# Attention, a dense layer and routed experts on one core: key and query steps one turn ahead, a second batch turned by VectorE, subtractions given to GpSimd

## Chip, core and metric

The kernel runs on one core of one Trainium2 chip. The metric is the device time of one execution in microseconds. Three runs of the kernel before gave 915.5, 917.96 and 918.49 us, with a median of 917.96 us.

## What is computed

```python
q, k, v: (4, 12, 448, 64)             # batch, heads, sequence, head_dim, float32
scores = q @ k.T / 8 - log(448)
x = sigmoid(scores) @ v               # -> (1792, 768)
h = x @ w_in                          # (768, 2048), float64 in memory
x2 = maximum(0.01 * h, h) @ w_out     # (2048, 768), float64 in memory
e = argmax(x2 @ w_gate)               # one of 8 experts for each token
y = maximum(x2 @ w1[e], 0) @ w2[e]    # (768, 1024), (1024, 768)
out = softmax(x2 @ w_gate)[e] * sigmoid(x2 @ w_ogate)[e] * y
```

Only the attention inputs, the two dense weights, the gates and the expert weights come from memory. All of the output is float32.

## The kernel before, in words

The 1792 tokens are four batches of 448. A batch goes through attention, the dense layer's first product (M1) and second product (M2), a routing step, and two products with the expert that is the commonest in the batch (M3, M4). A short loop at the end serves the tokens that want another expert.

Precise products are made of three fast ones. A tile is split into a hi part (rounded to the fast format) and a lo part (the rest), and `mm3` (lines 361 to 364) adds hi x hi, hi x lo and lo x hi. So each weight chunk of 128x768 or 128x640 is read (`raw`), copied by ScalarE to `whi`, and subtracted to `wlo`. Keys and queries are split in the same way: `kh`, `kl`, `qh`, `ql`.

Keys and queries must first be turned so that the head dimension lies on the partitions. For batches 0 and 1 TensorE does it (`turn`, line 422: four transposes into the PSUM tile `pst`). For batches 2 and 3 the load already lays out 32x32 blocks, and VectorE transposes these (`steps_T`, line 460: `kt`, `qt`).

Two ways of ordering stand side by side:

- `first_batches` (lines 978 to 1302) orders all work of batches 0 and 1 up to the end of batch 0's M2. It is a list of operations with an engine, a planned length and a due time; `_Plan.order` sorts them, and each engine gets its operations in that order. Here 34 chunks of the dense weights also change from float64 to float32: ScalarE makes `dw` from the loaded half chunk (line 1160), VectorE makes `raw` from it in three steps (lines 1165, 1168, 1171), GpSimd's queue stores the chunk for later batches (line 1181), and the chunk is split (lines 1200 and 1204). At the very start `heat` runs products of no use on TensorE (`hot`, line 1006).
- Later batches run as generators. The attention of batches 2 and 3 (`attention`, line 493) is spread over the products of earlier batches by `Filler`: for each step of the products, the attention may spend `ratio` times as much, and it pays with each of its `yield`s. One turn of it is a pair of heads: the scores of two chunks (`sc`, line 439), the previous pair's values (`pv`, line 452), the scores of the other two chunks; then four steps that turn and split the next pair's keys and queries. Routing (`routing`, line 610) goes forward one `yield` at a step of the products, and two in the last batch.

Each engine works through its queue in order; a wait at its head holds all that stands behind.

Of the kernel before, what the change touches and what calls it, by code (L numbers as in the profile page):

```python
# [9 lines left out]
F32 = mybir.dt.float32  # L10
# [8 lines left out]
P = 128  # L19
TP = 112  # L20
NCH = 4
# [98 lines left out]
def kernel(  # L120
# [13 lines left out]
    nc = tc.nc  # L134
# [132 lines left out]
    class Stream:  # L267
# [52 lines left out]
        def next(self):  # L320
            self.stage(2, self.ni)
            self.ahead()
            self.ni += 1
            return self.got.pop(self.ni - 1)
# [62 lines left out]

    SQ = 32

    def load_nat(nm, b, p):  # L390
        src = {"kn": k, "qn": q, "vn": v}[nm]
        if nm == "vn":
            a = nat_p.tile([TP, 2, NCH * D], F32, tag=nm, name=nm)
            if b >= 2:
                nc.sync.dma_start(a.rearrange("p h (c d) -> p h c d", c=NCH), src[b, 2 * p:2 * p + 2].rearrange("h (c p) d -> p h c d", c=NCH))
            else:
                nc.sync.dma_start(a, src[b, 2 * p:2 * p + 2].rearrange("h (p c) d -> p h (c d)", c=NCH))
        elif b >= 2:

            a = nat_p.tile([P, S // SQ, SQ], F32, tag=nm, name=nm)  # L400
            for j in range(P // SQ):
                i, f = divmod(j * SQ, D)
                nc.sync.dma_start(a[j * SQ:(j + 1) * SQ], src[b, 2 * p + i, :, f:f + SQ].rearrange("(n t) d -> t n d", t=SQ))
        else:
            a = nat_p.tile([TP, NCH, 2, D], F32, tag=nm, name=nm)
            for i in range(2):

                how = "(p c) d -> p c d" if nm == "kn" else "(c p) d -> p c d"
                nc.sync.dma_start(a[:, :, i, :], src[b, 2 * p + i].rearrange(how, c=NCH))
        nat[nm, b, p] = a  # L410

    def load_qk(b, p):
# [80 lines left out]
    def attention(b):  # L493


        st = {"at": {}}
        for _ in steps_T(b, 0, st):
            yield 0.4
        ahead_(load_qk, b, 2)
        prev = None  # L500
        for p in range(NP):
            nxt = {"at": {}}
            prep = steps_T(b, p + 1, nxt) if p + 1 < NP else iter(())
            room = None if p % 2 else rows_p.tile([TP, 2, 2, S], F32, tag="rows", name="ats")
            step_S(st, FRONT, room)
            if prev is not None:
                step_V(b, *prev, FRONT + BACK)
            step_S(st, BACK)
            for _ in range(4):
                yield C_E / 2  # L510
                next(prep, None)
            if p + 1 < NP:
                for _ in prep:
                    pass
                ahead_(load_qk, b, p + 3)
            prev = (p, st)
            st = nxt
        step_V(b, *prev, FRONT + BACK)
        yield C_V * 2
# [90 lines left out]
    def routing(b):  # L610
# [31 lines left out]
        yield  # L642
        rows_turn(b, xf[1], 1)
        xf[3] = rows_add(b, 3)
        yield
        yield
        yield
        cp = ps_t.tile([P, NCH, E], F32, tag="t", name="cp")
        nc.tensor.matmul(cp.rearrange("p c e -> p (c e)"), ones[:TP], eq.rearrange("p c e -> p (c e)"), start=True, stop=True)
        cnt = sm("cnt", [P, E])  # L650
# [327 lines left out]
    def first_batches():  # L978
# [4 lines left out]
        V = nc.vector  # L983
        L_QK, L_V, L_W64, L_W, LD_LAT = 1.3, 0.95, 1.55, 1.45, 2.0
        T_A, T_S2, T_V2, T_M = 0.4, 1.4, 1.8, 0.6
        A0 = 8.0
        HEAT = 24
        DEC = (40.0, 5.0)
        A_T = NP * 2 * (T_A + T_S2 + T_V2)
        D0 = A0 + A_T  # L990
# [15 lines left out]
            nc.tensor.matmul(hot.t[:, :P], ident, ident, start=True, stop=True)  # L1006

        for i in range(HEAT):
            pl.add(PE, 0.21, heat, uses=() if i == 0 else (hot,), new=() if i else (hot,), due=1e6)


        nats = {}

        def load(nm, b, p):
            s = pl.slot(nm, 2)
            nats[nm, b, p] = (s, pl.add(DMA, L_V if nm == "vn" else L_QK, lambda: load_nat(nm, b, p), new=(s,), lat=LD_LAT))

        def part(back):
            pv, vs, vop, b, p, at, sg, cs = back
# [17 lines left out]
        def attention_ops(b, t0, step):  # L1037
            for p in range(NP):
                for nm in ("kn", "qn", "vn"):
                    load(nm, b, p)  # L1040
            xs = pl.slot(f"x{b % 2}", 1)
            lows = low_of[b] = []
            behind = None
            for p in range(NP):
                def due(c):
                    return t0 + (p * NCH + c) * step


                stk, ready = {}, []
                for nm in "kq":  # L1050
                    ns, nop = nats[nm + "n", b, p]
                    ring = ("m", 2) if b == 0 and nm == "k" else ("t", 1)
                    ts = pl.slot("ps_" + ring[0], ring[1])
                    h, l = stk[nm] = [pl.slot(nm + x, 2) for x in "hl"]

                    def turn_(nm=nm, ts=ts, ring=ring, b=b, p=p):
                        ts.t = turn(nat.pop((nm + "n", b, p)), {"m": ps_m, "t": ps_t}[ring[0]], ring[0])

                    def thi(nm=nm, ts=ts, h=h):
                        h.t = stk_tile(nm + "h")  # L1060
                        nc.scalar.copy(h.t, ts.t)

                    def tlo(nm=nm, ts=ts, h=h, l=l):
                        l.t = stk_tile(nm + "l")
                        V.tensor_sub(l.t, ts.t, h.t.bitcast(F32))

                    o = pl.add(PE, T_A, turn_, deps=(nop,), uses=(ns,), new=(ts,))
                    o = pl.add(ACT, 0.5, thi, deps=(o,), uses=(ts,), new=(h,))
                    ready += [o, pl.add(DVE, 0.54, tlo, deps=(o,), uses=(ts, h), new=(l,))]
                four = (*stk["k"], *stk["q"])  # L1070
                pv = pl.slot("ps_v", 1)
                vs, vop = nats["vn", b, p]
                at, sg = {}, {}
                for cs in (FRONT, BACK):
                    sc = [pl.slot("ps_s", 2) for _ in cs]
                    new = list(sc)
                    deps, uses = list(ready), list(four)
                    back = behind
                    if cs == BACK:
                        new.append(pv)  # L1080
                        back = (pv, vs, vop, b, p, at, sg, FRONT)
                    if back:
                        deps += [back[2], *(back[6][c] for c in back[7])]
                        uses += [back[1], *(back[5][c] for c in back[7])]
                        if cs == FRONT:
                            uses.append(back[0])

                    def both(cs=cs, sc=sc, four=four, back=back):
                        for s_, t in zip(sc, scores(*(x.t for x in four), cs)):
                            s_.t = t  # L1090
                        if back:
                            part(back)

                    o = pl.add(PE, T_S2 + (T_V2 if back else 0.0), both, deps=deps, uses=uses, new=new, due=due(cs[1]))
                    if back:
                        last = o
                        if cs == FRONT:
                            finish(b, p - 1, back[0], last, xs, lows, due(0))
                    for c, s_ in zip(cs, sc):
                        at[c] = pl.slot("at", 4)  # L1100

                        def sig(s_=s_, a=at[c]):
                            a.t = squash(s_.t)

                        sg[c] = pl.add(ACT, 0.9, sig, deps=(o,), uses=(s_,), new=(at[c],))
                behind = (pv, vs, vop, b, p, at, sg, BACK)

            o = pl.add(PE, T_V2, lambda: part(behind), deps=(behind[2], *(behind[6][c] for c in BACK)),
                       uses=(behind[0], behind[1], *(behind[5][c] for c in BACK)), due=due(NCH) + 2.0)
            finish(b, NP - 1, behind[0], o, xs, lows, due(NCH) + 2.0)  # L1110
            return xs
# [80 lines left out]
        def chunk(j):  # L1192
            kk, n, _ = ws.src[j]
            got = fresh(j)
            hs, ls = his[j], los[j] = pl.slot("hi", 3), pl.slot("lo", 3)
            rs = raws[j]

            def hi():
                hs.t = whi_p.tile([P, kk, n], F32R, tag="hi", name="whi")
                nc.scalar.copy(hs.t, rs.v)  # L1200

            def lo():
                ls.t = wlo_p.tile([P, kk, n], F32R, tag="lo", name="wlo")
                V.tensor_sub(ls.t, rs.v, hs.t.bitcast(F32))  # L1204

            o = pl.add(ACT, 0.73, hi, deps=got, uses=(rs,), new=(hs,))
            return pl.add(DVE, 0.87, lo, deps=(o,), uses=(rs, hs), new=(ls,))


        nm = 0  # L1210
# [90 lines left out]
            ws.got[jj] = (his[jj].t, los[jj].t) if jj < stage[1] else raws[jj].v  # L1301
        gT[0] = None

    A_PE = NP * 2 * C_E + C_V + 1.6
    pace = [1]

    def tick(c):
# [40 lines left out]
    with tc.manual_schedule():  # L1348
        for b in range(0, B, 2):
            for i in range(2):  # L1350
                add_dense(b + i == 0)
            for i in range(2):
                add_exp(b + i)
        consts()
        first_batches()
        for b in range(0, B, 2):
# [59 lines left out]
```

## Time and profile before

| what | value |
|---|---|
| median of three runs | 917.96 us |
| the profiled execution's own time | 917.8 us |
| its span, first to last instruction | 916.2 us |
| TensorE busy | 889.9 us, 97% |
| VectorE busy | 506.1 us, 55% |
| ScalarE busy | 423.2 us, 46% |
| GpSimd busy | 59.4 us, 6% |
| granted TensorE clock, mean | 0.996 |

The span is 1.6 us shorter than the profiled execution's time. Busy time counts a matmul until its modelled end, and matmuls overlap in the pipeline; where one starts can be read from the start column. The list of waits shows for each engine what it stood idle for.

### The profile page before, as it was taken

How to read it: one execution, taken by the hardware profiler on the slowest of the kernel's cores; microseconds unless marked ns; L12 is line 12 of the kernel's file. 1: busy time of each engine (PE TensorE's matmuls, PEld its weight loads, DVE VectorE, ACT ScalarE, POOL GpSimd, SP SyncE). 2: the span in 40 equal slices, each digit the busy share in tenths (PEclk: the TensorE clock that was granted, in tenths of full speed). 3: DMA queues.
4: the chain of work that ended last, by engine and by line, in shares of the span. 5: the costliest groups of instructions: out<-in, count | busy, mean ns of one | idle time of the engine just before them, and what ended most of it. 6: DMA issues, size and time to landing. Idle time of an engine off the chain costs nothing.

```text
span 916.2 us, 13126 instructions
## 1 busy us (share of the span) xinstructions
PE 889.9 (97%) x4660; PEld 742.4 (81%) x4660; DVE 506.1 (55%) x994; ACT 423.2 (46%) x681; POOL 59.4 (6%) x94
## 2 busy tenths in 40 slices
PE   8799999999999999999999999999999999999996
PEld 6357877887899998787678777777989999889885
DVE  3748999852964327554334555432486432775343
ACT  5767676552444223445453656543345332233331
POOL 2000111100020000200000000000002100121000
PEclk9999999999999999999999999999999999999999
DMA  8984878872664333688346744232356434348433
GB/s 184 310 263 136 262 238 269 257 202 67 125 132 130 111 117 78 110 165 168 78 97 136 185 100 103 89 117 64 104 119 136 132 101 127 69 109 183 121 91 68
DMA packets 264773, 129.41 MB, mean 141 GB/s; under 512 B 172984, under 2 KB 249432, under 8 KB 264704
## 3 DMA queue, kind: packets, MB, share of 16 engines
q1 hardware_dynamic: 259584, 115.53, 51.0%
q0 software_dynamic: 4192, 12.89, 3.9%
q8 instruction: 38, 0.62, 0.3%
q14 instruction: 31, 0.25, 0.1%
q10 hardware_dynamic: 928, 0.11, 0.1%
HBM read 104.77 MB, written 23.77 MB: 140 GB/s over the span
## 4 chain that ended last, share of the span: by engine, by line
PE 75%; issue 8%; DVE 8%; DMA 2%; ACT 2%; SPq 0%; POOL 0%; POOLq 0%; ACTq 0%; DVEq 0%
PE psm L362 21%; PE psm L363 20%; PE psm L364 20%; PE pv L452 7%; PE sc L439 6%; DVE wlo L298 1%; DMA r64big<-in_moe_w_in_dram 1%; DMA r64big<-in_moe_w_out_dram 1%; DMA out_dram<-yt 1%; DVE wlo L1204 1%; DVE x2t L591 1%; DVE raw L1168 1%; PE lgT L561 1%; PE lgT L562 1%; DVE raw L1171 1%
## 5 line engine op out<-in xcount | busy, mean ns | idle before, releaser
L298 DVE TENSOR_TENSOR wlo<-raw,whi 128x768 fp32r<-128x768 f32 (+2 forms) x180 | 152.9, 854 | 84.8 <-ACT whi L290 83.3
L362 PE MATMUL psm<-gh,whi 128*128 128x448 f32 x528 | 193.3, 366 | 0.0
L364 PE MATMUL psm<-gh,wlo 128*128 128x448 f32 x528 | 191.1, 362 | 0.3 <-DVE wlo L298 0.3
L363 PE MATMUL psm<-gl,whi 128*128 128x448 f32 x528 | 191.3, 362 | 0.0
L290 ACT CAST whi<-raw 128x768 fp32r<-128x768 f32 (+2 forms) x180 | 135.6, 753 | 85.5 <-PE psm L363 71.9
L362 PEld LDWEIGHTS psm<-gh,whi 128*128 128x128 f32 x528 | 99.1, 188 | 14.4 <-issue 6.9
L362 PE MATMUL psm<-x0h,whi 128*128 128x448 f32 x288 | 107.1, 372 | 0.7 <-ACT x0h L1028 0.6
L362 PE MATMUL psm<-x1h,whi 128*128 128x448 f32 (+1 forms) x288 | 106.1, 369 | 0.0
L364 PEld LDWEIGHTS psm<-gh,wlo 128*128 128x128 f32 x528 | 98.9, 187 | 8.7 <-DVE wlo L298 1.6
L364 PE MATMUL psm<-x1h,wlo 128*128 128x448 f32 (+1 forms) x288 | 105.2, 365 | 0.0
L363 PE MATMUL psm<-x0l,whi 128*128 128x448 f32 x288 | 104.6, 363 | 0.4 <-DVE x0l L1032 0.4
L363 PE MATMUL psm<-x1l,whi 128*128 128x448 f32 (+1 forms) x288 | 104.8, 364 | 0.0
L364 PE MATMUL psm<-x0h,wlo 128*128 128x448 f32 x288 | 104.3, 362 | 0.0
L363 PEld LDWEIGHTS psm<-gl,whi 128*128 128x128 f32 x528 | 99.1, 188 | 5.6
L446 ACT ACTIVATE at<-sc,nbias 112x896 f32<-112x896 f32 x84 | 80.4, 1010 | 15.9 <-PE sc L439 15.7
L452 PE MATMUL pv<-at,vn 112*64 112x448 f32 x336 | 71.0, 550 | 0.0
L362 PEld LDWEIGHTS psm<-x0h,whi 128*128 128x128 f32 x288 | 54.1, 188 | 11.3 <-issue 4.8
L362 PEld LDWEIGHTS psm<-x1h,whi 128*128 128x128 f32 x288 | 54.1, 188 | 5.5 <-issue 0.6
L364 PEld LDWEIGHTS psm<-x1h,wlo 128*128 128x128 f32 x288 | 54.0, 188 | 4.6
L363 PEld LDWEIGHTS psm<-x1l,whi 128*128 128x128 f32 x288 | 54.0, 187 | 4.5
L363 PEld LDWEIGHTS psm<-x0l,whi 128*128 128x128 f32 x288 | 54.1, 188 | 4.1 <-DVE x0l L1032 0.9
L364 PEld LDWEIGHTS psm<-x0h,wlo 128*128 128x128 f32 x288 | 54.0, 187 | 4.0 <-DVE wlo L298 0.2
(218 smaller groups left out, 1051.4 us busy)
## 6 DMA issues: line engine op xcount, KB each, us to landing
raw<-wscr SPq DMA_DIRECT2D x66, 384.0 KB, 3.6
raw<-in_moe_w_dram SPq DMA_DIRECT2D x32, 384.0 KB, 3.9
raw<-in_moe_w_dram SPq DMA_DIRECT2D x48, 256.0 KB, 3.2
raw<-wscr SPq DMA_DIRECT2D x36, 320.0 KB, 2.9
r64big<-in_moe_w_in_dram SPq DMA_DIRECT2D x25, 384.0 KB, 5.3
wscr<-raw POOLq DMA_DIRECT2D x22, 384.0 KB, 5.4
r64big<-in_moe_w_out_dram SPq DMA_DIRECT2D x20, 384.0 KB, 5.3
vn<-in_v_dram SPq DMA_DIRECT2D x24, 224.0 KB, 3.7
```

What stands on the lines that cost most here:

```text
L290: nc.scalar.copy(hi, self.got[i])
L298: nc.vector.tensor_sub(lo, r, hi.bitcast(F32))
L362: nc.tensor.matmul(ps, wh, xh, start=first, stop=False)
L363: nc.tensor.matmul(ps, wh, xl, start=False, stop=False)
L364: nc.tensor.matmul(ps, wl, xh, start=False, stop=last)
L439: nc.tensor.matmul(t[:, i, :S], kk[own, ks], qq[own], start=(n == 0), stop=(n == 2))
L446: nc.scalar.activation(a, sc[:, :, :S], ACTF.Sigmoid, bias=nbias[:TP], scale=scale)
L452: nc.tensor.matmul(pv[own], vn[:, i, c * D:(c + 1) * D], at[c][:, i], start=(c == 0), stop=(c == NCH - 1))
L561: nc.tensor.matmul(lgT[b], wg_c[:, d], xh[:, d, :S], start=(d == 0), stop=False)
L562: nc.tensor.matmul(lgT[b], wg_c[:, d], xl[:, d, :S], start=False, stop=(d == KD - 1))
L591: nc.vector.transpose(t, xf)
L1168: V.scalar_tensor_tensor(t(), w(), 0x80000000, t(), ALU.bitwise_and, ALU.bitwise_or)
```

## The change

1. `TURNED = 1`: batch 1 too is loaded in 32x32 blocks (four DMAs for a key or query tile in place of two) and turned by VectorE (`swing`), so TensorE has 48 transposes less. The values of batch 1 are loaded in the layout of batches 2 and 3.
2. The lo parts of the dense weights within `first_batches` (34 chunks, and two of batch 1's) are subtracted by GpSimd, in the plan with 1.7 in place of VectorE's 0.87.
3. In `attention` a step of the next pair is made before each `yield` and no longer after it; the first pair's steps take 1.5 each in place of 0.4, with one more `yield` behind. `A_PE`, from which `ratio` follows, rises from 41.8 to 49.5.
4. Routing makes five `yield`s before the count `cp`, in place of three.
5. The first key and query tiles are loaded ahead of the constants, half by SyncE's queue and half by ScalarE's. `HEAT` falls from 24 to 14, `A0` from 8 to 6.

```diff
+    TURNED = 1
-    def load_nat(nm, b, p):
+    def load_nat(nm, b, p, by=(nc.sync, nc.sync)):
...
-            if b >= 2:
+            if b >= TURNED:
...
-                nc.sync.dma_start(a[:, :, i, :], src[b, 2 * p + i].rearrange(how, c=NCH))
+                by[i].dma_start(a[:, :, i, :], src[b, 2 * p + i].rearrange(how, c=NCH))
...
         for _ in steps_T(b, 0, st):
-            yield 0.4
+            yield 1.5
+        yield 1.5
...
             for _ in range(4):
+                next(prep, None)
                 yield C_E / 2
-                next(prep, None)
...
         xf[3] = rows_add(b, 3)
-        yield
-        yield
-        yield
+        for _ in range(5):
+            yield
...
-        A0 = 8.0
-        HEAT = 24
+        A0 = 6.0
+        HEAT = 14
...
-            pl.add(PE, 0.21, heat, uses=() if i == 0 else (hot,), new=() if i else (hot,), due=1e6)
+            pl.add(PE, T_A, heat, uses=() if i == 0 else (hot,), new=() if i else (hot,), due=1e6)
...
+                    def swing(nm=nm, ts=ts, b=b, p=p):
+                        ts.t = turn_p.tile([P, S], F32, tag=nm, name=nm + "t")
+                        V.transpose(ts.t, nat.pop((nm + "n", b, p)).rearrange("p n d -> p (n d)"))
...
-                    o = pl.add(PE, T_A, turn_, deps=(nop,), uses=(ns,), new=(ts,))
+                    o = pl.add(*((DVE, 0.6, swing) if own else (PE, T_A, turn_)), deps=(nop,), uses=(ns,), new=(ts,))
...
-                V.tensor_sub(ls.t, rs.v, hs.t.bitcast(F32))
+                nc.gpsimd.tensor_sub(ls.t, rs.v, hs.t.bitcast(F32))
...
-            return pl.add(DVE, 0.87, lo, deps=(o,), uses=(rs, hs), new=(ls,))
+            return pl.add("POOL", 1.7, lo, deps=(o,), uses=(rs, hs), new=(ls,))
...
-    A_PE = NP * 2 * C_E + C_V + 1.6
+    A_PE = NP * 2 * C_E + 2 * C_V + 7.5
...
+        for nm in ("kn", "qn"):
+            load_nat(nm, 0, 0, (nc.sync, nc.scalar))
         consts()
```

At the start TensorE's order before is 16 `hot`, the transposes of `kn`, 4 `hot`, those of `qn`, 4 `hot`, scores; now the `hot` counts are 7, 1 and 5, and the last one stands behind the first scores.

Three places in the order of instructions follow. First ScalarE in batch 0's attention, from the third pair of sigmoids (`at`, two chunks each) on. Before:

```order
L446 ACTIVATE at<-sc,nbias 112x896 x2
L1200 CAST whi<-raw 128x768
L446 ACTIVATE at<-sc,nbias 112x896 x2
L1061 CAST kh<-pst 128x448
L1061 CAST qh<-pst 128x448
L1160 ACTIVATE dw<-r64big 128x384 x3
L1028 CAST x0h<-pv 128x448
L446 ACTIVATE at<-sc,nbias 112x896 x2
```

The same stretch of ScalarE's queue in the changed kernel:

```order
L448 ACTIVATE at<-sc,nbias 112x896 x2
L1171 ACTIVATE dw<-r64big 128x384 x2
L1211 CAST whi<-raw 128x768
L448 ACTIVATE at<-sc,nbias 112x896 x2
L1068 CAST kh<-pst 128x448
L1068 CAST qh<-pst 128x448
L1171 ACTIVATE dw<-r64big 128x384 x2
L1171 ACTIVATE dw<-r64x 128x384
L1211 CAST whi<-raw 128x768
L1034 CAST x0h<-pv 128x448
L448 ACTIVATE at<-sc,nbias 112x896 x2
```

Two conversions of half chunks have moved in front of the fourth pair of sigmoids, and a `whi` in front of the fifth, behind three conversions as before.

Second GpSimd's queue in the changed kernel, from its first work for the weights on; before, only the stores (`wscr<-raw`) stood here, one after another:

```order
L1215 TENSOR_TENSOR wlo<-raw,whi 128x768 x3
L1192 DMA wscr<-raw 128x768 x8
L1215 TENSOR_TENSOR wlo<-raw,whi 128x768 x3
L1192 DMA wscr<-raw 128x768
L1215 TENSOR_TENSOR wlo<-raw,whi 128x768 x2
L1192 DMA wscr<-raw 128x768
```

The subtractions are now between the stores, the first three ahead of all stores.

Third VectorE in batch 2's attention, at the fourth pair of heads, whose queries' lo part is `ql`; `gl` and `wlo` belong to the expert product that runs beside it. Before:

```order
L460 STREAM_TRANSPOSE qt<-qn 128x448
L855 SCALAR_TENSOR_TENSOR gl<-psm,gh 128x448
L298 TENSOR_TENSOR wlo<-raw,whi 128x768
L463 TENSOR_TENSOR ql<-qt,qh 128x448
L482 TENSOR_TENSOR x0l<-pv,x0h 128x448
```

The same pair in the changed kernel:

```order
L462 STREAM_TRANSPOSE qt<-qn 128x448
L857 SCALAR_TENSOR_TENSOR gl<-psm,gh 128x448
L298 TENSOR_TENSOR wlo<-raw,whi 128x768
L465 TENSOR_TENSOR ql<-qt,qh 128x448
L462 STREAM_TRANSPOSE kt<-kn 128x448
L484 TENSOR_TENSOR x0l<-pv,x0h 128x448
```

On VectorE `ql` stands where it stood, but the next pair's `kt` now comes ahead of `x0l`. What the rows cannot show is that a `yield` now lies between `ql` and the scores that read it, so that TensorE has a piece of the product to do between them.

## Rows read from the trace of the kernel before

**Rows 1.** The page: span, and busy time of each engine.
```profile
span 916.2 us, 13126 instructions
PE 889.9 (97%) x4660; PEld 742.4 (81%) x4660; DVE 506.1 (55%) x994; ACT 423.2 (46%) x681; POOL 59.4 (6%) x94
```

**Rows 2.** Waits of TensorE: what it waited for, us, times, longest.
```profile
PE sc L439 <- ACT at L446: 5.1, 3, 4.0
PE sc L439 <- ACT qh L461: 2.8, 2, 1.5
PE sc L439 <- DVE ql L463: 1.9, 3, 1.5
...
PE cp L649 <- DVE eq L641: 1.4, 1, 1.4
...
PE sc L439 <- ACT ats L446: 1.0, 2, 0.5
PE sc L439 <- ACT qh L1061: 0.8, 1, 0.8
...
PE pst L422 <- DVE kl L1065: 0.4, 1, 0.4
```

**Rows 3.** Windows: length, busy of PE, PEld, DVE, ACT, POOL; clock, DMA share, GB/s.
```profile
20.00:40.00 20.00, 14.07 (x86) 7.40 (x88) 14.25 (x28) 15.43 (x24) 2.18 (x4) 0.91 1.03 299
...
80.00:200.00 120.00, 118.77 (x641) 95.22 (x640) 105.07 (x220) 78.74 (x137) 14.44 (x26) 1.00 0.81 247
200.00:217.00 17.00, 17.00 (x90) 13.07 (x88) 5.52 (x7) 6.48 (x9) 0.00 (x0) 1.00 0.26 83
```

**Rows 4.** Timeline of TensorE, first stretch: start, us, instruction, idle before.
```profile
6.92 0.55 PE L422 MATMUL pst<-ident,kn 112*128 112x112 f32 x4
...
8.21 0.55 PE L422 MATMUL pst<-ident,qn 112*128 112x112 f32 x4
...
9.59 0.46 PE L439 MATMUL sc<-qh,kh 64*112 64x448 f32 x2
...
32.82 0.72 PE L439 MATMUL sc<-qh,kh 64*112 64x448 f32 x2 [4.02 <-ACT at L446]
```

**Rows 5.** The two first loads of `qn`, issued at 2.4 and 3.0 us.
```profile
L409 SPq DMA_DIRECT2D qn<-in_q_dram x2: 490/551/612, 2.4 to 3.0; - x2
...
DMA to landing us min/median/max: 2.9/2.9/3.0
```

**Rows 6.** Timeline of ScalarE before the longest wait of TensorE ends.
```profile
30.89 0.55 ACT L1160 ACTIVATE dw<-r64big 128x384 f32<-128x384 f32 x1 [1.41 <-DVE raw L1168]
...
31.76 1.91 ACT L446 ACTIVATE at<-sc,nbias 112x896 f32<-112x896 f32 x2
```

**Rows 7.** Timeline of TensorE around a group of transposes of batch 1.
```profile
108.52 0.55 PE L422 MATMUL pst<-ident,kn 112*128 112x112 f32 x4
108.84 0.45 PE L362 MATMUL psm<-x0h,whi 128*128 128x448 f32 x1
```

**Rows 8.** Timeline of VectorE ahead of the scores of batch 2's fourth pair.
```profile
434.74 0.95 DVE L298 TENSOR_TENSOR wlo<-raw,whi 128x768 fp32r<-128x768 f32 x1
435.61 0.62 DVE L463 TENSOR_TENSOR ql<-qt,qh 128x448 fp32r<-128x448 f32 x1
```

**Rows 9.** Groups of VectorE, 80 to 200 us: count, busy us, mean ns.
```profile
L1204 DVE TENSOR_TENSOR wlo<-raw,whi 128x768 fp32r<-128x768 f32 (+1 forms) x25 | 22.5, 902 | 3.2 <-ACT whi L1200 2.8
...
L1246 DVE TENSOR_TENSOR g<-t,psm 128x448 f32<-128x448 f32 x14 | 8.6, 615 | 0.2
```

**Rows 10.** Line 460: VectorE's transposes, ns min, median, max.
```profile
L460 DVE STREAM_TRANSPOSE kt<-kn x12: 635/638/639, 377.9 to 604.4; 128x448 f32<-128x448 f32 x12
```

**Rows 11.** Timeline of GpSimd: its longest instruction that is no DMA.
```profile
794.85 0.76 POOL L756 MEMSET xm<- 32x769 f32 x1
```

**Rows 12.** DMA issues: count, KB each, median us to landing.
```profile
kn<-in_k_dram SPq DMA_DIRECT2D x24, 112.0 KB, 4.4
...
kn<-in_k_dram SPq DMA_DIRECT2D x48, 56.0 KB, 3.2
```

More of the change, by code (lines that the diff above doesn't have):

```diff
@@ L397, in load_nat @@
                 nc.sync.dma_start(a, src[b, 2 * p:2 * p + 2].rearrange("h (p c) d -> p h (c d)", c=NCH))
-        elif b >= 2:
+        elif b >= TURNED:
             a = nat_p.tile([P, S // SQ, SQ], F32, tag=nm, name=nm)
@@ L1015, in load @@
             s = pl.slot(nm, 2)
-            nats[nm, b, p] = (s, pl.add(DMA, L_V if nm == "vn" else L_QK, lambda: load_nat(nm, b, p), new=(s,), lat=LD_LAT))
+            if (nm, b, p) in nat:
+                o = pl.add(DMA, L_QK / 2, lambda: None, new=(s,), due=0.0, lat=LD_LAT)
+            else:
+                o = pl.add(DMA, L_V if nm == "vn" else L_QK, lambda: load_nat(nm, b, p), new=(s,), lat=LD_LAT)
+            nats[nm, b, p] = (s, o)
         def part(back):
@@ L1051, in attention_ops @@
                     ns, nop = nats[nm + "n", b, p]
-                    ring = ("m", 2) if b == 0 and nm == "k" else ("t", 1)
-                    ts = pl.slot("ps_" + ring[0], ring[1])
+                    own = b >= TURNED
+                    ring = (nm, 1) if own else ("m", 2) if b == 0 and nm == "k" else ("t", 1)
+                    ts = pl.slot(("turn_" if own else "ps_") + ring[0], ring[1])
                     h, l = stk[nm] = [pl.slot(nm + x, 2) for x in "hl"]
```

## The prediction

> **What bounds the kernel now.** I read the page first. TensorE is busy for 889.9 of 916.2 us [rows 1], so the kernel is bound by TensorE, and only two things can shorten it: less work on TensorE, or fewer of the 26.3 us in which it stands idle. A faster VectorE, ScalarE or GpSimd is worth something only where TensorE waits for it.
>
> So the second view is the list of TensorE's waits [rows 2]. The reader is to see that the waits are few and have names. Scores wait 5.1 us for sigmoids (`at`), 4.0 of them at once. Scores of the later batches wait 2.8 us for `qh` and 1.9 us for `ql`. The count `cp` waits 1.4 us. Batch 1's keys and queries cost 0.8 and 0.4 us of waiting. Another 1.0 us goes to `ats`, the first sigmoids of a batch.
>
> The third view is the table of stretches [rows 3]. From 20 to 40 us TensorE is busy for 14.07 of 20 us, with the DMA engines at a share of 1.03: there the transfers are full and TensorE is not. From 80 to 200 us TensorE is busy for 118.77 of 120 us and VectorE for 105.07: VectorE has little left, but TensorE hardly waits for it. From 200 us on VectorE has 11.5 of 17 us free.
>
> **The change part by part.**
>
> *Transposes.* 12 groups of four leave TensorE. A group that starts at 108.52 us is followed by a product at 108.84 [rows 7], so it costs 0.32 us, and 12 x 0.32 = 3.8 us go. VectorE gets 12 transposes of 0.64 us [rows 10] for them. The two waits that belonged to them, 0.8 for `qh` and 0.4 for `kl` [rows 2], can go too, since no PSUM tile is shared any longer; I take 1.0 of 1.2, with 0 and 1.2 as bounds. The loads for them are smaller and twice as many: 56 KB lands after 3.2 us, 112 KB after 4.4 [rows 12]. SyncE issues some 0.55 us a piece [rows 5], so 24 more issues are 13 us of its queue, spread over 200 us, and the conversions of the dense weights stand behind them. They are loaded two pairs ahead, and that hides them; without this cover, within the stretch of full DMA engines, they would cost up to the difference of 2 x 3.2 and 4.4 us, 2.0 us, once. That is within the bounds of the next part.
>
> *The start.* The last `qn` load is issued at 3.0 us and lands 2.9 us later [rows 5], yet its transposes start at 8.21, behind the useless products, and the scores at 9.59 [rows 4]. With half of the issues on ScalarE's queue the last issue is some 1.1 us earlier, and with 8 useless products ahead in place of 20 the transposes can start at 5.5 to 6. I take 2.4 us for that. Behind it stands the wait of 4.0 us, which ends at 32.82 [rows 4]. Its cause is ScalarE's queue: the sigmoids at 31.76 stand behind a conversion that waited 1.41 us for VectorE [rows 6], and that one behind loads. In the new order three conversions and a `whi` stand before the same sigmoids, and two conversions before the pair ahead of them. So I do not take this wait as removed: loads decide it, they come earlier by what the start gives, and the gain may be 0.6 us beyond that. The granted clock is 0.91 over these 20 us, and the matmul pair at 32.82, after 4.02 us of idleness, takes 0.72 us where 0.46 is usual [rows 4]: that is 1.8 us of clock lost at the lower of the two levels, 1.2 in place of 2.4 GHz. Together I take 3.0 us. The bounds are 0 (loads set the pace and the head start is lost) and 8.2 (2.4, the whole 4.0, and the 1.8).
>
> *Subtractions on GpSimd.* VectorE loses 25 of 0.90 us, 22.5 us, between 80 and 200 us [rows 9]. No row shows GpSimd with two inputs. The lower bound is its memset of 769 columns at 0.76 us [rows 11], which only writes; the upper is three times that, 2.3 us, for two reads and a write in turn. I take 1.5, nearer to the memset doubled. GpSimd is busy for 14.44 of these 120 us [rows 3]; 25 x 1.5 = 37.5 us more leave it half idle, and even 57.5 us fit. As VectorE was not what TensorE waited for, the relief is worth nothing by itself. The chunk is ready 0.6 us later than before; three buffers hide that, and I count it once, where the first product starts: +0.6 us.
>
> By the Trainium skill's "GPSIMD Engine Reference", section 3.1, the same operation takes GpSimd 4497 ns where VectorE takes 2293. An estimate from that ratio is 1.8 us for a subtraction here, and the sum with it would be 0.3 us higher.
>
> *One turn ahead.* Scores of the fourth pair wait for `ql`, which runs at 435.61, directly behind a `wlo` [rows 8], because it was given out just before them. Now a `yield` of 1.6 lies between. At the new ratio, `A_PE` over three products of 8 x 6 steps of 0.57 (82.1) by 1.08, 49.5 / 82.1 x 1.08 = 0.65, it is paid with 1.6 / 0.65 = 2.5 us of products. All five long waits of this kind are at most 1.5 us [rows 2], so the work that hides them is longer. 2.8 + 1.9 = 4.7 us go. The bounds are 3.0 (for the pair above `gl` and `wlo` still come first, and half of it may stay) and 5.5. The 1.0 us for `ats` stays, since it is the first turn's own chain of scores and sigmoids.
>
> *Routing.* Two more `yield`s are one step of the products in the last batch, where two are made at a time: three matmuls, 0.6 us of the 1.4. I take 0.6; bounds 0 and 1.4.
>
> **Sum.** 3.8 + 1.0 + 3.0 + 4.7 + 0.6 - 0.6 = 12.5 us less than the profiled execution's own 917.8 us: 905.3. That execution is 0.2 us from the median of the runs shown, so I predict 905.
>
> **The rivals.**
>
> *VectorE and GpSimd shut each other out.* As a mechanism: while GpSimd subtracts, VectorE cannot do what reads two tiles of SBUF. Without the `wlo`, VectorE has 105.07 - 22.5 = 82.6 us of work between 80 and 200 us, and 8 transposes add 5.1: 87.7. With 25 subtractions of 1.5 us that nothing overlaps it is 125.2 us for a stretch of 120, in which chunks already come just in time. That is 5.2 us back, 910.5; I put it at 911. For it speaks that the stretch is the fullest of the kernel on VectorE; against it, that the gains elsewhere stay and that VectorE has room after 200 us.
>
> The Trainium skill, "SBUF — State Buffer", section "Who interferes with whom", states this as a rule: a VectorE instruction with two SBUF inputs contends with a GpSimd instruction that reads SBUF, and the loser waits for the whole instruction. No row here shows the two together, so it bears on this rival alone, and with its sister page's 1.8 us the rival would be at 917.
>
> *Slower than before.* The same place at the upper price. At 2.3 us the sum is 87.7 + 57.5 = 145.2 us, 25 us more than the stretch; with `g` (8.6 us, one input in PSUM [rows 9]) and the transposes running beside it, 11.5. The middle is 18 us: 905 + 18 = 923. It decides from a shut-out of 1.8 us on, where 25 x 1.8 + 87.7 passes 120 by the 12.5 us of the gains. Against it: 0.76 us for 769 columns.
>
> *The head start is lost.* Loads fill the DMA engines at 20 to 40 us; if they set the pace from the first microsecond on, the start brings nothing and the sum is 908.
>
> *Waits only move.* The change does not do what it says: `ql` still comes last behind `gl` and `wlo`, batch 1's transposes on VectorE come behind decoding and scores wait for them. The 4.7 and 1.0 us stay, the start is lost: 914 to 917, say 916. Against it, the covers worked out above.
>
> **How the numbers follow.** Forecast 0.55 (its own range 899 to 910), lost head start 0.13 (908), shut-out 0.17 (911), slower 0.07 (923), waits only move 0.08 (916). The range 897 to 914 holds the first three but for their ends, 0.80. A difference of 0.3%, 2.8 us, is about what a measurement of this kernel can tell from none; so faster means below 915.2: 0.54 + 0.13 + 0.15 + 0.02 = 0.84. Within 0.3%: 0.08. Slower: 0.08.
>
> **What would show it.** In the changed kernel's trace the scores' waits for `qh` and `ql` are gone from TensorE's list. The first scores start at about 7 us in place of 9.59. Transposes of batch 1 stand on VectorE, and the first product of batch 1 (`x1h`) starts some 7 us earlier than before. TensorE still waits for `at` somewhere before 40 us, for 2 to 4 us. GpSimd's subtractions are spaced by 1.5 us where three follow one another, and VectorE is busy for about 88 us of a stretch of the same work. The prediction is wrong if VectorE's other instructions take visibly longer than before while GpSimd subtracts, if TensorE's list has a new wait for `wlo`, or if the stretch up to 40 us ends as late as before.

## The result and the profile after

The changed kernel takes 929.59 us (median of four runs, 927.87 to 930.52); the kernel before, in the four runs beside it, takes 917.61. The ratio is 1.0132, with a 95% interval of 1.0117 to 1.0146. It is slower by 12 us; 905 us was predicted. The profiled execution took 927.87 us.

The page of the changed kernel, to be held against [rows 1]:

```profile
span 926.3 us, 13072 instructions
PE 888.0 (96%) x4592; PEld 739.5 (80%) x4592; DVE 515.9 (56%) x970; ACT 421.0 (45%) x681; POOL 122.7 (13%) x130
```

TensorE is busy 1.9 us less than before and the span is 10.1 us longer, so the time went into waits. One line of the page deserves a second look: VectorE gave away 36 subtractions and took up 12 transposes, yet it is busy for 515.9 us where it was busy for 506.1.

TensorE's list of waits in the changed kernel (what it waited for, us in total, times, longest):

```profile
PE sc L441 <- ACT at L448: 12.4, 6, 4.7
PE psm L362 <- DVE g L1257: 9.4, 5, 3.9
...
PE cp L651 <- DVE eq L644: 0.8, 1, 0.8
```

Against [rows 2], the waits for `qh` and `ql` of the later batches are gone, as predicted, and the count's wait has shrunk from 1.4 to 0.8. But the wait for sigmoids has grown from 5.1 to 12.4 us, and there is a wait that was not there at all: 9.4 us for `g`, the first product's result behind its leak, which VectorE makes.

More than a third of the sigmoid wait is one place: 4.7 us at 54.85 us. ScalarE's sigmoids there stand directly behind this conversion of a half chunk, which waited for its load:

```profile
53.35 0.54 ACT L1171 ACTIVATE dw<-r64big 128x384 f32<-128x384 f32 x1 [3.79 <-DMA r64big<-in_moe_w_in_dram]
```

The table of stretches of the changed kernel (columns as in [rows 3]):

```profile
20.00:40.00 20.00, 13.88 (x81) 6.68 (x80) 16.98 (x26) 15.34 (x25) 5.99 (x4) 0.91 0.98 254
40.00:60.00 20.00, 13.16 (x68) 6.40 (x65) 12.74 (x28) 9.23 (x16) 3.60 (x7) 0.91 0.91 274
...
120.00:140.00 20.00, 15.33 (x75) 11.62 (x74) 16.72 (x26) 12.34 (x22) 7.60 (x7) 0.92 0.64 195
140.00:160.00 20.00, 20.00 (x100) 15.13 (x100) 16.97 (x32) 12.50 (x23) 8.99 (x8) 0.90 0.72 217
...
80.00:200.00 120.00, 108.76 (x554) 85.44 (x550) 107.33 (x186) 72.57 (x128) 54.27 (x45) 0.97 0.69 209
```

From 80 to 200 us TensorE was busy for 118.77 us and now is for 108.76. VectorE, without its 25 subtractions, is still busy for 107.33, and for fewer instructions (186 in place of 220). The granted clock falls to 0.92 and 0.90 between 120 and 160 us.

Where one of the new waits comes from is seen in the timelines around 135 us. TensorE first:

```profile
134.31 0.36 PE L363 MATMUL psm<-x0l,whi 128*128 128x448 f32 x1
134.51 0.36 PE L364 MATMUL psm<-x0h,wlo 128*128 128x448 f32 x1
138.81 0.74 PE L362 MATMUL psm<-x0h,whi 128*128 128x448 f32 x1 [3.94 <-DVE g L1257]
139.35 0.57 PE L363 MATMUL psm<-x0l,whi 128*128 128x448 f32 x1
139.73 0.57 PE L364 MATMUL psm<-x0h,wlo 128*128 128x448 f32 x1
```

VectorE in the same stretch:

```profile
127.39 3.02 DVE L1264 TENSOR_TENSOR gl<-g,gh 128x448 fp32r<-128x448 f32 x1
...
130.87 0.55 DVE L1176 TENSOR_SCALAR raw<-dw 128x384 uint32<-128x384 uint32 x2
...
135.11 0.60 DVE L1076 STREAM_TRANSPOSE qt<-qn 128x448 f32<-128x448 f32 x1
135.64 2.12 DVE L1176 TENSOR_SCALAR raw<-dw 128x384 uint32<-128x384 uint32 x2
137.68 0.55 DVE L1179 SCALAR_TENSOR_TENSOR raw<-dw,raw 128x384 uint32<-128x384 uint32 x1
138.15 0.61 DVE L1257 TENSOR_TENSOR g<-t,psm 128x448 f32<-128x448 f32 x1
```

And GpSimd:

```profile
135.78 1.83 POOL L1215 TENSOR_TENSOR wlo<-raw,whi 128x768 fp32r<-128x768 f32 x1 [0.85 <-ACT whi L1211]
```

VectorE works without a gap from 127.39 us on, so `g` is late only because of what stands ahead of it. The two shifts at 135.64 take 2.12 us; the pair at 130.87, with no subtraction beside it, takes 0.55. They end at 137.76, 0.15 us behind GpSimd's subtraction, which began at 135.78. TensorE then stands for 3.94 us and comes back with matmuls that start 0.38 us apart, where 0.20 was usual. From 137.0 to 143.8 us the granted clock is 0.50: the lower of the two levels, after idleness, as in [rows 4].

### The profile page after: what moved, and what is told of

It is laid out like the page before. It is cut to its first block, busy times and chain, and to the rows that moved or that the text cites. A ratio compares the mean times of both kernels' runs of the same rounds, so it can differ in the third digit from the quotient of the medians.

```text
span 926.3 us, 13072 instructions
## 1 busy us (share of the span) xinstructions
PE 888.0 (96%) x4592; PEld 739.5 (80%) x4592; DVE 515.9 (56%) x970; ACT 421.0 (45%) x681; POOL 122.7 (13%) x130
## 4 chain that ended last, share of the span: by engine, by line
PE 72%; DVE 10%; issue 9%; DMA 3%; ACT 3%; SPq 1%; POOL 0%; DVEq 0%; POOLq 0%; ACTq 0%
PE psm L362 20%; PE psm L364 19%; PE psm L363 19%; PE pv L454 6%; PE sc L441 6%; DMA r64big<-in_moe_w_in_dram 2%; DVE raw L1179 1%; DVE raw L1176 1%; DVE x2t L594 1%; DVE wlo L298 1%; ACT dw L1171 1%; SPq L411 1%; DVE gl L1264 1%; DVE xf L587 1%; DVE raw L1182 1%
## 5 line engine op out<-in xcount | busy, mean ns | idle before, releaser
L362 PE MATMUL psm<-x0h,whi 128*128 128x448 f32 x288 | 108.3, 376 | 10.7 <-DVE g L1257 9.4
L1215 POOL TENSOR_TENSOR wlo<-raw,whi 128x768 fp32r<-128x768 f32 (+1 forms) x36 | 65.2, 1814 | 124.8 <-ACT whi L1211 109.4
L731 POOL DMA_INDIRECT lists<-tok,ii x16 | 16.4, 1023 | 449.3 <-DVE cf L736 417.5
```

The costliest lines, as they stand in the source:

```text
L362: nc.tensor.matmul(ps, wh, xh, start=first, stop=False)
L731: nc.gpsimd.indirect_dma_start(flat, bass.IndirectOffsetOnAxis(ap=ii[:, c], axis=0), tok[:TP, b, c:c + 1], None, bounds_check=E * LS - 1, ...
L1215: nc.gpsimd.tensor_sub(ls.t, rs.v, hs.t.bitcast(F32))
```

## The experiments

Four theories stood. **A:** a GpSimd instruction that reads two tiles and VectorE's instructions of certain kinds cannot run together, and each such meeting is paid by VectorE's queue. **B:** batch 1's smaller and more numerous loads crowd the DMA queues. **C:** the lo parts are only later than before, or GpSimd's stores behind them are. A fourth, weaker reading came with A: the order was written for lengths that no longer hold, and another order would pay less.

The kernel before took 918.63, 919.23 and 919.04 us (medians) beside the first four, the next four and the last four runs; the ratios are to those. The three groups ran on three chips, and beside the changed kernel the kernel before took 917.61 us; so between groups a difference of medians is good to some 1.6 us.

**Lo parts back on VectorE**, and nothing else:

```diff
-                nc.gpsimd.tensor_sub(ls.t, rs.v, hs.t.bitcast(F32))
+                V.tensor_sub(ls.t, rs.v, hs.t.bitcast(F32))
...
-            return pl.add("POOL", 1.7, lo, deps=(o,), uses=(rs, hs), new=(ls,))
+            return pl.add(DVE, 0.87, lo, deps=(o,), uses=(rs, hs), new=(ls,))
```

> The changed kernel with the lo parts of the first stage's weights back on VectorE (plan 0.87); all else as changed. Theory A (GpSimd's subtractions and VectorE's two-input instructions shut each other out, and that costs the stretch from 80 us on some 11 us and a part of the first 60 us): about 914 us, 912 to 918, and the first stage ends some 13 us earlier than in the changed kernel. Theory B (batch 1's smaller and more numerous loads crowd the DMA engines and hold the conversions of the weights, the subtractions are harmless): 926 us or more.

909.08 us, ratio 0.9898 (0.9875 to 0.9922), below all that was expected. The whole loss and more is in this one edit: 929.59 - 909.08 = 20.5 us (21.5 by the ratios). Without it the change is a gain of 1%.

**Batch 1 turned by TensorE again** (`TURNED = 2`), subtractions left on GpSimd:

> The changed kernel with batch 1's keys and queries again loaded whole and turned by TensorE; the subtractions stay on GpSimd. Theory A: TensorE's 3.8 us of transposes come back and the shut-out stays, so 929 us, 926 to 934. Theory B: the stage recovers, about 918 us, 914 to 921.

934.70 us, ratio 1.0165 (1.0138 to 1.0193): 5.1 us worse than the changed kernel, a little more than A allowed. B falls here: the smaller loads belong to a part that helps.

**Both of these edits**, so that steps ahead, routing and the start remain:

> The changed kernel with both of these undone: what is left are the steps one turn ahead, the two yields of routing and the new start. Both theories: 909 us, 906 to 913 (6.4 us less in the later batches than before, and some 2 us at the start). If it is above 915, the new order of the first 60 us is a cause of its own.

912.35 us, ratio 0.9933 (0.9913 to 0.9953). Against the first run, turning on VectorE is worth 3.3 us (TensorE's wait for sigmoids is 3.6 us here and 7.2 in the first run, so a part of what the transposes gave came back as waiting; what causes it is not shown); against the second, GpSimd's subtractions cost 22.4 us without it.

**The kernel before with steps one turn ahead and the routing's `yield`s alone** (parts 3 and 4 of the change):

> The kernel before with the steps one turn ahead, the higher share of attention and the two yields of routing alone. Both theories: 911 us, 910 to 913, 6.4 us less than before, all of it in batches 2 and 3. A rival says that the waits come back elsewhere: 915 or more.

912.77 us, ratio 0.994 (0.9922 to 0.9959): 5.9 us for the two. The start, which separates this run from the one above, brings 0.4 us, with intervals that overlap.

How the subtraction costs 20 us is read from VectorE's groups between 80 and 200 us. The columns are count, busy us, mean ns of one, idle before. In the changed kernel:

```profile
L1179 DVE SCALAR_TENSOR_TENSOR raw<-dw,raw 128x384 uint32<-128x384 uint32 (+1 forms) x45 | 33.2, 752 | 0.4
L1176 DVE TENSOR_SCALAR raw<-dw 128x384 uint32<-128x384 uint32 (+1 forms) x45 | 21.0, 494 | 3.7 <-POOL wlo L1215 3.4 <-ACT dw L1171 0.3
L1182 DVE SCALAR_TENSOR_TENSOR raw<-r64big,raw 128x384 uint32<-128x384 uint32 (+1 forms) x36 | 19.7, 563 | 0.1
L1264 DVE TENSOR_TENSOR gl<-g,gh 128x448 fp32r<-128x448 f32 x16 | 14.9, 937 | 2.1 <-ACT gh L1261 2.1
L1257 DVE TENSOR_TENSOR g<-t,psm 128x448 f32<-128x448 f32 x15 | 9.1, 610 | 5.3 <-ACT t L1253 5.3
```

The same groups with the lo parts on VectorE:

```profile
L1179 DVE SCALAR_TENSOR_TENSOR raw<-dw,raw 128x384 uint32<-128x384 uint32 (+1 forms) x52 | 26.2, 525 | 0.7
L1215 DVE TENSOR_TENSOR wlo<-raw,whi 128x768 fp32r<-128x768 f32 (+1 forms) x26 | 23.5, 903 | 1.3 <-ACT whi L1211 0.8
L1182 DVE SCALAR_TENSOR_TENSOR raw<-r64big,raw 128x384 uint32<-128x384 uint32 (+1 forms) x42 | 20.9, 526 | 0.1
L1176 DVE TENSOR_SCALAR raw<-dw 128x384 uint32<-128x384 uint32 (+1 forms) x52 | 16.5, 339 | 1.7 <-ACT dw L1171 1.6
L1264 DVE TENSOR_TENSOR gl<-g,gh 128x448 fp32r<-128x448 f32 x15 | 9.3, 621 | 0.0
L1257 DVE TENSOR_TENSOR g<-t,psm 128x448 f32<-128x448 f32 x14 | 8.6, 613 | 0.3 <-ACT t L1253 0.3
```

The reader is to go down the means. `raw<-dw,raw` and `gl`, which read two tiles of SBUF, last 1.4 and 1.5 times as long beside GpSimd; so does the shift `raw<-dw`, which reads one (1.5). `g`, which reads one tile and PSUM, has not changed (610 against 613), and neither have the transposes.

But `raw<-r64big,raw` also reads two tiles, and its mean has hardly moved (526 to 563). The trace says why, when each instruction is held against GpSimd's subtractions by its start and end. Of all `raw<-r64...` steps in the stretch only 5 of 45 ran while a subtraction did; these took 1104 ns on average, the other 40 took 517. Of `raw<-dw,raw` 13 of 45 met one (1333 against 516 ns), of the shifts 9 of 45 (1115 against 338), of `gl` 6 of 16 (1478 against 613). Nine of the 15 `g` met one too and stayed at 609. So the price falls on the single instruction that meets a subtraction, up to 2.2 us for a decoding step (its own 0.5 and nearly a whole subtraction) and 3.0 for a `gl`; those that meet none are as long as in the first run.

Added up, 45 x 0.227 + 45 x 0.155 + 36 x 0.037 + 16 x 0.316 = 23.6 us, and two smaller groups, `raw<-r64x,raw` and `kl`, add 1.3 us each. The 26 subtractions that VectorE was spared took 23.5. The same is seen over the whole run: with 36 subtractions more, VectorE is busy for 512.1 us in the first run, against 515.9 in the changed kernel.

```profile
PE 884.0 (97%) x4592; PEld 738.0 (81%) x4592; DVE 512.1 (56%) x1006; ACT 421.3 (46%) x681; POOL 58.8 (6%) x94
```

VectorE has not been relieved at all; its work now also comes in lumps, at times that the order does not know of.

**Reads without the lateness.** To part A from C, the lo parts stay on VectorE, and GpSimd subtracts pieces of the same tiles into a tile that nobody reads, six pieces of 96 columns a chunk (five for the narrower ones):

```diff
...
+            def ghost():
+                gt = ghost_p.tile([P, 96], F32, tag="gh", name="ghost")
+                for c in range(kk):
+                    nc.gpsimd.tensor_sub(gt, rs.v[:, c, :96], hs.t[:, c, :96].bitcast(F32))
...
+            pl.add("POOL", 1.7, ghost, deps=(o,), uses=(rs, hs))
             return pl.add(DVE, 0.87, lo, deps=(o,), uses=(rs, hs), new=(ls,))
```

> The first experiment's kernel (lo parts on VectorE) with subtractions on GpSimd added whose result nobody reads: after each hi part of the 36 chunks, four to six subtractions of 128x96 of the same raw and hi tiles, about 1.8 us of GpSimd in all for a chunk. The output is not changed, and no chunk waits for them. Theory A (VectorE's two-input instructions and GpSimd's reads shut each other out): VectorE's instructions get longer by some 0.2 us each while these run, and as VectorE also has its own 0.87 us for each lo part, the time is 925 us or more, against 909.1 without them. Theory C (the cost is that a chunk's lo part is ready later and queues behind stores on GpSimd's queue): 908 to 911, no change.

929.15 us, ratio 1.0105 (1.0081 to 1.0128). Some 20 us are lost again, though no lo part is later by way of GpSimd's queue, and between 80 and 200 us VectorE waits for only 1.0 us until GpSimd has read a tile. VectorE between 80 and 200 us, and GpSimd's pieces over the whole run:

```profile
L1180 DVE SCALAR_TENSOR_TENSOR raw<-dw,raw 128x384 uint32<-128x384 uint32 (+1 forms) x44 | 25.0, 589 | 0.4
...
L1271 DVE TENSOR_TENSOR gl<-g,gh 128x448 fp32r<-128x448 f32 x16 | 12.9, 811 | 0.0
...
L1221 POOL TENSOR_TENSOR ghost<-raw,whi 128x96 f32<-128x96 f32 x204 | 115.9, 568 | 81.3 <-ACT whi L1212 67.0 <-POOL ghost L1221 0.4
```

**Writes alone.** The same place and the same wait, but in place of the subtractions a copy of one column and ten memsets:

```diff
-                for c in range(kk):
-                    nc.gpsimd.tensor_sub(gt, rs.v[:, c, :96], hs.t[:, c, :96].bitcast(F32))
+                nc.gpsimd.tensor_copy(gt[:, 0:1], hs.t[:, 0, 0:1].bitcast(F32))
+                for c in range(10):
+                    nc.gpsimd.memset(gt, 0.0)
```

> The same, but in place of the subtractions GpSimd copies one column of the hi tile and then only writes: ten memsets of 128x96 for a chunk, about 1.8 us of GpSimd. The output is not changed. Theory A, if it is GpSimd's reading that shuts VectorE's second input out: near 909, at most 913. If any work of GpSimd does it: as much as the subtractions, 925 or more. Theory C: 908 to 911.

912.23 us, ratio 0.9925 (0.9896 to 0.9953). By the ratios that is 2.5 us above the first run, and the intervals overlap. The stretch from 80 to 200 us, and two groups of VectorE in it:

```profile
80.00:200.00 120.00, 120.00 (x633) 96.70 (x630) 109.11 (x229) 81.67 (x143) 81.17 (x317) 1.00 0.80 233
...
L1180 DVE SCALAR_TENSOR_TENSOR raw<-dw,raw 128x384 uint32<-128x384 uint32 (+1 forms) x51 | 25.4, 518 | 0.6
...
L1177 DVE TENSOR_SCALAR raw<-dw 128x384 uint32<-128x384 uint32 (+1 forms) x51 | 16.7, 348 | 7.2 <-DMA wscr<-raw 7.2
```

GpSimd is busy for 81.17 us here (51.3 of them memsets, 17.8 the copies, the rest stores), more than the 54.27 of the changed kernel, and TensorE for 120.00 of 120. VectorE's means are the undisturbed ones. GpSimd's stores even come late enough that VectorE waits 7.2 us for them, and TensorE does not notice. So neither a busy GpSimd nor late stores cost the 20 us: C falls, and A stands with the addition that it is GpSimd's reading of tiles that counts, not its writing.

**An order made for the lengths that hold.** The changed kernel, with the plan told what its trace showed; no instruction is added or taken away:

```diff
-            return pl.add("POOL", 1.7, lo, deps=(o,), uses=(rs, hs), new=(ls,))
+            return pl.add("POOL", 2.0, lo, deps=(o,), uses=(rs, hs), new=(ls,))
...
-                    o2 = pl.add(DVE, 0.27, shift, deps=(o, *prev[1:]), uses=(dws, *((rs,) if h else ())), new=() if h else (rs,))
+                    o2 = pl.add(DVE, 0.45, shift, deps=(o, *prev[1:]), uses=(dws, *((rs,) if h else ())), new=() if h else (rs,))
```

and likewise `sign` 0.47 to 0.66, `tail_bits` 0.47 to 0.54, `glo_` 0.54 to 0.85.

> The changed kernel, with the plan told the lengths that its trace shows: 2.0 for a subtraction on GpSimd, 0.45, 0.66 and 0.54 for VectorE's three conversion steps, 0.85 for gl. Only the order changes. If a part of the loss comes from an order made for lengths that do not hold: 918 to 925, against 929.6. If VectorE simply has too little time (theory A alone): 927 to 932.

918.86 us, ratio 1.0007 (0.999 to 1.0025). A line of its list of TensorE's waits:

```profile
PE psm L362 <- DVE g L1257: 3.7, 2, 2.1
```

And two groups of VectorE from 80 to 200 us:

```profile
L1179 DVE SCALAR_TENSOR_TENSOR raw<-dw,raw 128x384 uint32<-128x384 uint32 (+1 forms) x46 | 29.6, 672 | 0.1
L1182 DVE SCALAR_TENSOR_TENSOR raw<-r64big,raw 128x384 uint32<-128x384 uint32 (+1 forms) x36 | 26.4, 755 | 0.0
```

929.59 - 918.86 = 10.7 us of the 20.5 come back by order alone, the wait for `g` falling from 9.4 to 3.7. The meetings have not become fewer or cheaper, they fall on other instructions: `raw<-dw,raw` and `gl` are shorter than in the changed kernel (672 and 723 ns), `raw<-r64big,raw` and the shift are longer (755 and 553), a subtraction on GpSimd takes 1901 ns, and VectorE is busy for 522.1 us in all, 6.2 more than in the changed kernel. So about half of the price hung on the order, that is on which instructions the meetings fell on and what stood behind them, and not on how long the meetings were in sum. Even so it is no better than the kernel before.

**The start as before**, in the kernel of the first run (`HEAT`, `A0` and the first loads as before):

> The first experiment's kernel without the new start: A0, HEAT and the first loads as before. If the start's gain of 1.4 us at the first scores is eaten by the loads that follow, 909 us, 907 to 911; if it lasts, 911 to 912.

911.97 us, ratio 0.9919 (0.9889 to 0.9948): 2.9 us above the first run, but on another chip (1.9 us by the ratios), and against the 0.4 us above. The pair was therefore repeated side by side below.

**Where the price is paid: the first product's 16 chunks on GpSimd, the other 20 on VectorE, and the other way round.**

```diff
-                nc.gpsimd.tensor_sub(ls.t, rs.v, hs.t.bitcast(F32))
+                (nc.gpsimd if j < KF else V).tensor_sub(ls.t, rs.v, hs.t.bitcast(F32))
...
-            return pl.add("POOL", 1.7, lo, deps=(o,), uses=(rs, hs), new=(ls,))
+            return pl.add(*(("POOL", 1.7) if j < KF else (DVE, 0.87)), lo, deps=(o,), uses=(rs, hs), new=(ls,))
```

> The changed kernel, with GpSimd subtracting the 16 chunks of the first product and VectorE the other 20; plan 1.7 or 0.87 accordingly. If every subtraction on GpSimd costs the same, 16/36 of the 20.5 us come: 918 us. If it costs only where VectorE is also decoding and TensorE waits for it already (the stretch up to about 130 us), most of it comes: 922 to 928 us.

> The mirror image: VectorE subtracts the 16 chunks of the first product, GpSimd the 20 after them. If every subtraction costs the same, 20/36 of the 20.5 us: 920 to 921 us. If only the first part counts, since VectorE has room later: 909 to 912 us, no worse than with VectorE doing all of them (909.1).

924.64 us, ratio 1.0063 (1.004 to 1.0086), and 913.70 us, ratio 0.9944 (0.9923 to 0.9966). Beside them ran a repetition with all lo parts on VectorE:

> The changed kernel with all lo parts on VectorE, a second time, beside the next run on the same chip: 909 us. If the changed start is worth its 2.9 us, it is again about 2.9 us below the next run.

910.54 us, ratio 0.9902 (0.9883 to 0.9921). So the first 16 cost 14.1 us, 0.9 each; the other 20 cost 3.2 us, 0.16 each. (913.70 us lies above the 909 to 912 expected if only the first part counts.) Together that is 17.3 us, less than the 20.5 (19.1 against this repetition) of all 36. TensorE's longest waits in sum, with the first product's chunks on GpSimd, are those for `g`:

```profile
PE psm L362 <- DVE g L1257: 8.2, 4, 3.9
```

and VectorE's decoding and `gl` with the second product's:

```profile
L1179 DVE SCALAR_TENSOR_TENSOR raw<-dw,raw 128x384 uint32<-128x384 uint32 (+1 forms) x50 | 26.4, 546 | 0.7
L1176 DVE TENSOR_SCALAR raw<-dw 128x384 uint32<-128x384 uint32 (+1 forms) x50 | 23.2, 484 | 5.6 <-POOL wlo L1215 4.6 <-ACT dw L1171 0.8
...
L1264 DVE TENSOR_TENSOR gl<-g,gh 128x448 fp32r<-128x448 f32 x16 | 9.8, 618 | 0.0
```

The price is not one per subtraction. In the first product VectorE also makes `g` and `gl`, for which TensorE waits in the end, and the lengthened decoding stands ahead of them in the queue. In the second product there is no `g`: the shift is lengthened there too (484 ns), and the only long wait of TensorE that is new is one of 2.3 us for sigmoids, at 166.78 us. That it is the missing `g` which makes the second product cheap is argued, not shown: VectorE also has more time there. With all lo parts on VectorE (the first run) it is busy for 59.37 of the 60 us from 80 to 140, and for 52.02 of the 60 us after that.

**The start once more**, on the same chip as the three above:

> The same with the first loads, HEAT and A0 as before the change, a second time: 912 us if the start is worth 2.9 us, 909 to 910 if it is worth nothing, as the pair of steps alone and steps with the start (912.8 and 912.4) said.

910.83 us, ratio 0.9934 (0.9906 to 0.9963): 0.3 us above its partner by the medians, but 2.9 by the ratios, as two of its seven executions took 915.68 and 918.42 us. By the medians the three pairs give 0.4, 2.9 (across two chips) and 0.3 us, by the ratios 0.6, 1.9 and 2.9, and in each pair the intervals overlap. So the start is worth between nothing and 3 us, and these runs tell no more. TensorE's timeline of the partner with the changed start shows that a part of the head start is lost again:

```profile
7.35 0.46 PE L441 MATMUL sc<-qh,kh 64*112 64x448 f32 x2
...
11.77 0.58 PE L424 MATMUL pst<-ident,kn 112*128 112x112 f32 x4 [1.57 <-DMA kn<-in_k_dram]
12.28 0.71 PE L441 MATMUL sc<-qh,kh 64*112 64x448 f32 x2
```

and of the one with the start as before:

```profile
9.29 0.46 PE L441 MATMUL sc<-qh,kh 64*112 64x448 f32 x2
...
11.65 0.46 PE L441 MATMUL sc<-qh,kh 64*112 64x448 f32 x2
```

The first scores come 1.9 us earlier, and the second scores 0.6 us later: the next `kn` is not there yet, and its transposes wait 1.57 us for it.

The best version is the changed kernel with its lo parts left on VectorE: 909.08 and 910.54 us, 1.0% below the kernel before both times. Its list of TensorE's waits has one long line left, and none for `g`:

```profile
PE sc L441 <- ACT at L448: 7.2, 4, 2.6
```

## Why the prediction was wrong, step by step

| step of the prediction | predicted | measured | from |
|---|---|---|---|
| subtractions on GpSimd | +0.6 | +20.5 | first run against the changed kernel |
| one turn ahead, and routing | -4.7 - 0.6 | -5.9 | those parts alone |
| transposes and their waits | -3.8 - 1.0 | -3.3 | first and third run |
| the start | -3.0 | -0.3 to -2.9, not resolved | three pairs |

With a start of 0.4 the measured terms make 20.5 - 5.9 - 3.3 - 0.4 = 10.9 us; 12.0 were measured.

**The step that failed** is the one on GpSimd: "As VectorE was not what TensorE waited for, the relief is worth nothing by itself", with +0.6 us for lateness as the whole cost. Its price for one subtraction was not what was wrong: 1.5 us was taken, within 0.76 to 2.3, and the trace has 1.81 over the whole run:

```profile
L1215 POOL TENSOR_TENSOR wlo<-raw,whi 128x768 fp32r<-128x768 f32 (+1 forms) x36 | 65.2, 1814 | 124.8 <-ACT whi L1211 109.4 <-PE sc L441 15.3
```

What was wrong was to add that price to an engine with free time, as if it had no other payer. VectorE paid some 26 us for being spared 23.5, TensorE waited for what VectorE had in its queue, and the clock fell in the longest of those waits. The prediction had named this as a sign that it is wrong: other instructions of VectorE visibly longer while GpSimd subtracts. The difference of the two profiled spans, 926.3 - 907.2 = 19.1 us, can be put together from the tables of stretches. The kernel with the lo parts on VectorE has

```profile
20.00:40.00 20.00, 14.77 (x87) 6.61 (x87) 15.74 (x32) 15.81 (x25) 1.71 (x3) 0.91 1.05 279
40.00:60.00 20.00, 15.98 (x82) 8.87 (x80) 14.72 (x31) 11.43 (x18) 2.16 (x4) 0.91 0.94 285
...
80.00:200.00 120.00, 120.00 (x634) 97.28 (x634) 111.39 (x234) 80.48 (x141) 14.85 (x26) 1.00 0.83 246
```

so the changed one idles 0.9 + 2.8 us more up to 60 us and 11.2 us more from 80 to 200. Of the 6.8 us at half clock after 137.0 it worked for 5.0, which lost 2.5. That makes 17.4 of 19.1. Most of the 2.8 us is the wait at 54.85 us shown above, 4.7 us where the first run waits for 2.1; GpSimd subtracts nothing between 39.8 and 80 us. Whether earlier meetings delayed the load behind that wait is not shown.

**The rivals.** "Slower than before" named the right mechanism and the point from which it decides, a shut-out of 1.8 us; the subtraction measured 1.81. It got a chance of 0.07, because one row for a memset that only writes was held against it, and the runs show that a write is just the case that does no harm. Its 923 was still too low, and it came from the upper price of 2.3 us: with the measured 1.81 its own sum gives 87.7 + 45.3 - 120 = 13 us, so 918 us (the prediction writes 917 for 1.8). It charged the lengthening as a sum over 120 us with room at the end, while the trace shows single meetings of up to 3 us in front of `g` that an average hides; half of the price went with the order. That VectorE has room after 200 us did not help, since most of the price is paid in the first product. "The head start is lost" came true beside it in part, as far as the three pairs tell.

The Trainium skill, "SBUF — State Buffer", section "Who interferes with whom", has the rule by which it came out, and the traces agree with it: instructions with two SBUF inputs took 1104 to 1478 ns beside a subtraction and 516 to 613 without one, the one with a PSUM input stayed at 609, and GpSimd's memsets, which only write, lengthened nothing. The same section says that a one-input instruction in a mode that uses both ports contends as well, and names `tensor_scalar` among those that can enter one; the shift is a `tensor_scalar`, and took 1115 ns beside a subtraction where 338 is usual. That it ran in such a mode no trace here shows. That half of the rule was not drawn on in the prediction; only both together cover all three decoding steps.

**Where it was right.** One turn ahead and routing measured 5.9 us where 5.3 were predicted, and the waits named for it are gone from the list. Turning on VectorE measured 3.3 where 4.8 were predicted. TensorE still lost 0.5 us there with the transposes back (a wait for `kl`), so the transposes' own 3.8 and the waits' 1.0 are not told apart by these runs. The prediction's 0.55 us for an issue did not hold where the DMA engines are full: four issues for `kn` from 45.58 us on took 4.78 us of SyncE's queue in the changed kernel (DMA share 0.91 in that stretch), and the four at 44.64 us in the first run 2.60 (0.94). The first scores came at 8.16 us in the changed kernel's trace, where about 7 was said:

```profile
8.16 0.46 PE L441 MATMUL sc<-qh,kh 64*112 64x448 f32 x2
```

What the start was worth, nothing to 3 us, lay in the lower part of the prediction's own bounds (0 to 8.2): a part of it is lost at the load of the next `kn`. The first product of batch 1 (`x1h`) starts at 240.4 us in the changed kernel and at 223.9 in the one before, 16.5 us later where 7 us earlier was said: the loss lies ahead of it.

**What stays open:** which part of the remaining 10 us, after the order knows the lengths, is VectorE's added work and which is meetings that no fixed order can foresee; whether the second product is cheap for want of a `g` or because VectorE has time there; and what the start is worth.

## What to carry to other kernels

Moving an operation to an idle engine is not free when it makes the relieved engine's other instructions longer, as a subtraction on GpSimd did here. Before such a move is priced, list the kinds of instruction that the relieved engine keeps: here those that read two tiles of SBUF and the shift were held up, those with a PSUM input were not. Charge each meeting to that engine's queue, at the length of the other engine's instruction. Look for it in the stretch where the bottleneck engine reads that queue's results, at what stands ahead of them, and not in the average load of 120 us. When an order is worked out from planned lengths, a change of engine changes lengths that are not in the diff: plan again with those of the new trace before the idea is judged.

## What was not expected of the hardware

The shift, which reads one tile, is held up as much as the others: 0.55 us for two became 2.12 beside one subtraction of 1.83 us. Two engines that meet in this way gave back nothing: 23.5 us of work taken from VectorE became some 26 us of longer instructions there. 268 memsets and 26 small copies on GpSimd, 69.1 us in 120, left VectorE's means where they were (518 and 348 ns against 525 and 339).
